# Gradients of keys, values and the input x in three interleaved stages, with memory rows padded to full tiles

## The chip, the cores and the metric

One core of one Trainium2 chip runs the whole program. The metric is the device time of one execution in microseconds, lower is better. The kernel before takes 8813.72 us (median of 4 runs beside the changed kernel).

## The reference, cut to what matters

The program computes a gated mix of two attentions over 2048 tokens, and all gradients. Branch A is attention with 32 heads and one set of keys and values. Branch B, which this change concerns, walks through 64 segments of 32 tokens; each segment attends to itself (causally) and to 8 memory rows that the segment before it wrote.

```python
for s in range(n_seg):
    xs = x[:, s * seg_len:(s + 1) * seg_len, :].copy()
    h = jnp.concatenate([mem, xs], axis=1)
    q, k, v = ...                       # projections of h, 32 heads of 128
    p = _softmax(masked scores, axis=-1)
    o = ...                             # p @ v, output projection to 576
    mem = o[:, :M, :].copy()
    outs.append(o[:, M:, :])
...
return g * a + (1 - g) * b              # then the gradients of all inputs
```

The stage at hand comes after the backward walk through the memory rows. For each tile of 128 tokens and each half of the heads (a **unit**; there are 16 x 2 = 32) it forms the gradients of keys and values as sums of two parts, from the tokens' own queries and from the memory rows' queries, stores them, transposes them, and multiplies the gradients of q, k and v by the transposed weights into the gradient of the input x.

## The kernel before

In the sums, the part of the tokens is a matmul over 128 rows, the part of the memory rows one over the 32 rows that belong to a group of four heads. They alternate, both adding into the same place:

```python
for tt in range(NTT):
    dxa = ...; load; dxa = gwb * dz + dxa                # gate's term, VectorE
    px = psum.tile([P, 640], F32, name="x_b", bufs=1)
    for r in range(2):
        # ... five loads of 512 KB, one buffer each; keys, values, memory rows
        for w, lt, rt, ml, mr, sc in (("v", ...), ("k", ...)):
            dt = sp.tile([P, 4, 4, E], BF16, name="g_dt", bufs=1)
            for g in range(4):
                rs = slice(32 * g, 32 * g + 32)
                pk = psum.tile([P, 4, E], F32, name="x_p", bufs=4)
                for i in range(4):
                    self.mm(pk[:, i, :], lhsT=lt[:, g, i, :], rhs=rt[:, g, i, :], start=True, stop=False)
                    self.mm(pk[:, i, :], lhsT=ml[rs, i, :], rhs=mr[rs, i, :], start=False, stop=True, tp=(32 * g, 0))
                nc.scalar.mul(dt[:, g], pk[:], sc)
                self.tr4(psum, "x_tr", lambda i: dt[:, g, i, :], de[:, g], use="v")
            nc.gpsimd.dma_start(self.DX[w][tok, hc], ...)
        for n, w in enumerate("qvk"):                    # input gradients, 16 heads each
            # ... 512 and 64 columns per head, added into px
    # ... dx = dxa + px, stored
```

The order of the instructions on each engine is set by the compiler's scheduler; some stages of this program fix TensorE's order by hand (`self.chain = True`), this one did not.

The softmax here doesn't subtract the row's maximum and nothing guards it: scores larger than these inputs give would overflow.

## Time and profile before

| | kernel before |
|---|---|
| median time | 8813.72 us |
| profiled execution | 8801.6 us |
| stage of this change | 7013.0 to 7970.3 us: 957.3 us, 29.9 us per unit |
| TensorE's granted clock in the stage | 0.78 |
| TensorE busy by the records | 953.98 us of 957.3 |
| DMA share, rate | 0.60, 183 GB/s |

The busy share of TensorE says little here, because each record is counted from start to a modelled end, and records overlap (in the prediction's timeline, records of 0.23 us start 0.16 us apart). What counts are the distances between starts, and the clock that the chip granted. The prediction below shows both.

### The profile page before, as it was taken

How to read it: one execution, taken by the hardware profiler on the slowest of the kernel's cores; microseconds unless marked ns; L12 is line 12 of the kernel's file. 1: busy time of each engine (PE TensorE's matmuls, PEld its weight loads, DVE VectorE, ACT ScalarE, POOL GpSimd, SP SyncE). 2: the span in 40 equal slices, each digit the busy share in tenths (PEclk: the TensorE clock that was granted, in tenths of full speed). 3: DMA queues.
4: the chain of work that ended last, by engine and by line, in shares of the span. 5: the costliest groups of instructions: out<-in, count | busy, mean ns of one | idle time of the engine just before them, and what ended most of it. 6: DMA issues, size and time to landing. Idle time of an engine off the chain costs nothing. (4 is left out here: it accounts for less than half of the span.)

```text
span 8801.6 us, 210293 instructions
## 1 busy us (share of the span) xinstructions
PE 8158.4 (93%) x89816; PEld 3903.5 (44%) x89816; DVE 4321.7 (49%) x6659; ACT 3835.0 (44%) x7412; POOL 1184.8 (13%) x3062
## 2 busy tenths in 40 slices
PE   6999999999999979978999899979999799997999
PEld 2222222222222234435555566647777555554444
DVE  4889898898888924432333455542222111113000
ACT  3788787787777823332222355542222111112000
POOL 4100001000010014420000133320000011112000
PEclk9999999999999989979999999989999877776999
DMA  2000000000000045542211588883333466666444
GB/s 89 1 6 1 6 6 1 6 1 6 6 1 1 1 146 230 231 178 86 60 59 59 175 267 263 260 284 104 99 98 97 167 189 190 185 187 221 149 149 144
DMA packets 615950, 969.83 MB, mean 110 GB/s; under 512 B 187545, under 2 KB 406946, under 8 KB 594850
## 3 DMA queue, kind: packets, MB, share of 16 engines
q1 hardware_dynamic: 540978, 672.32, 24.4%
q0 software_dynamic: 72720, 282.73, 8.6%
q8 instruction: 702, 11.50, 0.5%
q14 instruction: 238, 1.95, 0.1%
q10 hardware_dynamic: 1312, 1.33, 0.0%
HBM read 552.06 MB, written 404.10 MB: 109 GB/s over the span
## 5 line engine op out<-in xcount | busy, mean ns | idle before, releaser
L1355 DVE TENSOR_TENSOR a_U<-a_d,a_E 128x1024 bf16<-128x1024 f32 x2048 | 2474.3, 1224 | 302.3 <-ACT a_E L1350 233.1
L1350 ACT ACTIVATE a_E<-a_s 128x512 bf16<-128x512 f32 x4096 | 2237.5, 595 | 564.7 <-PE a_s L79 478.9
L79 PE MATMUL a_s<-a_qaug,a_kmask 128*128 128x512 bf16 x2048 | 704.1, 388 | 54.7 <-ACT a_tk L1432 24.5
L79 PE MATMUL a_s<-a_kmask,a_qaug 128*128 128x512 bf16 x2048 | 697.3, 384 | 25.9 <-ACT a_E L1350 9.6
L79 PE MATMUL w_acc<-w_col,w_h 128*128 128x512 bf16 (+1 forms) x2400 | 526.1, 381 | 0.9 <-DMA w_col<-dqx 0.9
L79 PEld LDWEIGHTS <-d_g 128*32 128x32 bf16 x18432 | 494.6, 97 | 26.4 <-issue 9.9
L63 DVE CAST p_tok<-p_pb 128x512 bf16<-128x512 f32 x384 | 265.3, 692 | 318.4 <-PE p_pb L79 318.4
L79 PE MATMUL a_d<-a_doT,a_vaugT 32*128 32x512 bf16 x2048 | 401.5, 389 | 0.1
L79 PE MATMUL a_d<-a_vaugT,a_doaT 32*128 32x512 bf16 x2048 | 397.6, 385 | 0.0
L65 ACT COPY p_em<-p_tr 128x512 bf16<-128x512 bf16 x384 | 225.0, 586 | 357.7 <-PE p_tr L84 357.5
L1442 POOL TENSOR_TENSOR a_otok<-a_tk,a_rl 128x144 bf16<-128x144 f32 x64 | 27.5, 429 | 2525.4 <-DVE a_rl L1441 2525.4
L79 PEld LDWEIGHTS <-w_h 128*128 128x128 bf16 (+1 forms) x2400 | 237.4, 100 | 289.4 <-issue 24.2
L79 PEld LDWEIGHTS <-a_vaugT 32*128 32x128 bf16 x2048 | 96.4, 91 | 572.7 <-issue 572.6
L79 PEld LDWEIGHTS <-a_doaT 32*128 32x128 bf16 x2048 | 95.9, 91 | 538.0 <-issue 537.6
L65 ACT CAST c_tm<-c_pb 128x512 bf16<-128x512 f32 x192 | 112.5, 586 | 471.4 <-PE c_pb L79 471.2
L1042 ACT ACTIVATE g_dt<-x_p 128x512 bf16<-128x512 f32 x256 | 142.7, 599 | 355.5 <-DMA dvx<-g_dt 216.0
L63 DVE CAST c_tm<-c_pb 128x512 bf16<-128x512 f32 x192 | 132.9, 692 | 313.6 <-PE c_pb L79 309.2
L63 DVE CAST w_o<-w_acc 128x512 bf16<-128x512 f32 (+1 forms) x60 | 41.4, 690 | 481.3 <-PE w_acc L79 448.6
L79 PEld LDWEIGHTS <-c_mT 128*32 128x32 bf16 x7680 | 187.9, 96 | 190.9 <-DVE c_mT L396 25.4
L79 PEld LDWEIGHTS <-a_kmask 128*128 128x128 bf16 x2048 | 125.1, 97 | 313.8 <-issue 305.9
L79 PEld LDWEIGHTS <-p_xT 128*128 128x128 bf16 (+1 forms) x1920 | 154.8, 97 | 218.0 <-issue 87.7
L65 ACT CAST w_o<-w_acc 128x512 bf16<-128x512 f32 (+1 forms) x60 | 35.1, 585 | 496.6 <-PE w_acc L79 496.6
(482 smaller groups left out, 13797.5 us busy)
## 6 DMA issues: line engine op xcount, KB each, us to landing
xt_k<-p_tok SPq DMA_DIRECT2D x16, 1024.0 KB, 4.0
xe_k<-p_em POOLq DMA_DIRECT2D x16, 1024.0 KB, 5.5
xs_k<-p_seg POOLq DMA_DIRECT2D x64, 256.0 KB, 4.3
xt_v<-p_tok SPq DMA_DIRECT2D x16, 1024.0 KB, 3.9
xe_v<-p_em POOLq DMA_DIRECT2D x16, 1024.0 KB, 5.6
xs_v<-p_seg POOLq DMA_DIRECT2D x64, 256.0 KB, 2.9
xt_q<-p_tok SPq DMA_DIRECT2D x16, 1024.0 KB, 4.2
xe_q<-p_em POOLq DMA_DIRECT2D x16, 1024.0 KB, 5.8
```

The lines of the kernel that those rows point to most:

```text
L63: nc.vector.tensor_copy(out, in_)
L65: nc.scalar.copy(out, in_)
L79: self.follow(self.nc.tensor.matmul(out, lhsT, rhs, start=start, stop=stop, tile_position=tp, skip_group_check=True))
L1042: nc.scalar.mul(dt[:, g], pk[:], sc)
L1350: nc.scalar.activation(ex[:, j, :], s[:, :], ACT.Exp, scale=SCALEA)
L1355: nc.vector.tensor_tensor(out=u[:], in0=d[:], in1=ex[:], op=ALU.mult)
L1442: nc.gpsimd.tensor_tensor(out=osl, in0=v[:, :, :, o0:o0 + DA], in1=rl[:].to_broadcast([P, 4, 2, DA]), op=ALU.mult)
```

## The change

The intent is to keep TensorE dense. The memory rows are copied into tiles that are zero outside their own 32 rows, so that each second matmul also uses all 128 rows. The work of a unit goes through three stages (sums of 4 heads; transposes of the step before; input gradients of the step before that), interleaved with the memory part of the next unit, in an enforced order. The five large loads come in halves with two buffers, the output accumulator has two, and the stores of the key and value gradients are issued by ScalarE instead of GpSimd.

```diff
+        pad = {}
+        for nm in ("mdo", "mq"):
+            pad[nm] = keep.tile([P, 4, 4, E], BF16, name="g_pad_" + nm)
+            nc.gpsimd.memset(pad[nm][:], 0.0)
@@ ... cut ... @@
+        def own_rows(U, nm, g):
+            rs = slice(32 * g, 32 * g + 32)
+            nc.scalar.copy(pad[nm][rs, g], U[nm][rs])
@@ ... cut ... @@
+        def sums(U, w, g):
+            lt, rt, ml, nm, sc = ("eq", "dot", "eM", "mdo", 1.0) if w == "v" else ("sq", "qt", "sM", "mq", SCALEB)
+            pk = bank([P, 4, E])
+            for i in range(4):
+                self.mm(pk[:, i, :], lhsT=U[lt, g // 2][:, g % 2, i, :], rhs=U[rt, g // 2][:, g % 2, i, :], start=True, stop=False)
+                self.mm(pk[:, i, :], lhsT=U[ml][:, i, :], rhs=pad[nm][:, g, i, :], start=False, stop=True)
+            if g % 2 == 0:
+                U["d" + w] = sp.tile([P, 2, 4, E], BF16, name="g_dt" + w, bufs=2)
+            dt = U["d" + w]
+            nc.scalar.mul(dt[:, g % 2], pk[:], sc)
+            if g % 2:
+                tok = slice(U["tt"] * P, (U["tt"] + 1) * P)
+                c0 = U["r"] * 2048 + (g // 2) * 1024
+                nc.scalar.dma_start(self.DX[w][tok, c0:c0 + 1024], dt[:].rearrange("p g i e -> p (g i e)"))
+            return dt[:, g % 2]
@@ ... cut ... @@
+        def prefetch(tt):
+            t = dxa[tt] = sp.tile([P, D], F32, name="g_dxa", bufs=2)
+            nc.sync.dma_start(t[:], self.dxA_dram[tt * P:(tt + 1) * P, :])
+            nc.vector.scalar_tensor_tensor(out=t[:], in0=gwb[:], scalar=self.dz_all[:, tt:tt + 1], in1=t[:],
                                            op0=ALU.mult, op1=ALU.add)
@@ ... cut ... @@
-                for w, lt, rt, ml, mr, sc in (("v", ld["eq"], ld["dot"], eM, mdo, 1.0), ("k", ld["sq"], ld["qt"], sM, mq, SCALEB)):
-                    dt = sp.tile([P, 4, 4, E], BF16, name="g_dt", bufs=1)
-                    de = sp.tile([P, 4, 4, P], BF16, name=f"g_d{w}e", bufs=1)
-                    for g in range(4):
-                        rs = slice(32 * g, 32 * g + 32)
-                        pk = psum.tile([P, 4, E], F32, name="x_p", bufs=4)
-                        for i in range(4):
-                            self.mm(pk[:, i, :], lhsT=lt[:, g, i, :], rhs=rt[:, g, i, :], start=True, stop=False)
-                            self.mm(pk[:, i, :], lhsT=ml[rs, i, :], rhs=mr[rs, i, :], start=False, stop=True, tp=(32 * g, 0))
-                        nc.scalar.mul(dt[:, g], pk[:], sc)
-                        self.tr4(psum, "x_tr", lambda i: dt[:, g, i, :], de[:, g], use="v")
-                    nc.gpsimd.dma_start(self.DX[w][tok, hc], dt[:].rearrange("p g i e -> p (g i e)"))
-                    em[w] = de
-                for n, w in enumerate("qvk"):
-                    for i in range(4):
-                        for g in range(4):
-                            h = 16 * r + 4 * g + i
-                            st, sp_ = n + r + i + g == 0, n == 2 and r == 1 and i + g == 6
-                            for lo, hi in ((0, 512), (512, D)):
-                                self.mm(px[:, lo:hi], lhsT=em[w][:, g, i, :], rhs=self.WT[w][:, h, lo:hi], start=st, stop=sp_)
@@ ... cut ... @@
+        for n, U in enumerate(units):
+            N = units[n + 1] if n + 1 < len(units) else None
+            if U["r"] == 0:
+                prefetch(U["tt"])
+            if N:
+                load_keys(N)
+            for g in range(4):
+                if g == 0:
+                    loads(U, 1)
+                if g == 2 and N:
+                    loads(N, 0)
+                if g == 3 and n + 2 < len(units):
+                    load_memory(units[n + 2])
+                for w in "vk":
+                    dt = sums(U, w, g)
+                    if N:
+                        if (g, w) == (0, "v"):
+                            memory_rows(N, "mdo", "do")
+                        if (g, w) == (0, "k"):
+                            memory_rows(N, "mq", "q")
+                        if (g, w) == (1, "k"):
+                            memory_scores(N)
+                        if (g, w) == (2, "k"):
+                            memory_gradients(N)
+                        own_rows(N, "mdo" if w == "v" else "mq", g)
+                    inputs(U, "q", g, (0, 1) if w == "v" else (2, 3), U["dqe", g // 2][:, g % 2])
+                    if done:
+                        done[-1].append(columns(done[-1][3]))
+                    if len(done) > 1:
+                        V, w2, g2, _, de = done.pop(0)
+                        inputs(V, w2, g2, range(4), de)
+                    done.append([U, w, g, dt])
+        done[-1].append(columns(done[-1][3]))
+        for V, w2, g2, _, de in done:
+            inputs(V, w2, g2, range(4), de)
+        self.chain = False
```

More of the change, by code (lines that the diff above doesn't have):

```diff
@@ L987, in b_x_gradients @@
         NTT = self.NTT
+        units = [dict(tt=tt, r=r) for tt in range(NTT) for r in range(2)]
         gwb = keep.tile([P, D], BF16, name="g_gwb")
         nc.sync.dma_start(gwb[:], self.gate_w.partition_broadcast(P))
-        for tt in range(NTT):
-            tok = slice(tt * P, (tt + 1) * P)
-            dxa = sp.tile([P, D], F32, name="g_dxa", bufs=2)
-            nc.sync.dma_start(dxa[:], self.dxA_dram[tok, :])
-            nc.vector.scalar_tensor_tensor(out=dxa[:], in0=gwb[:], scalar=self.dz_all[:, tt:tt + 1], in1=dxa[:],
-                                           op0=ALU.mult, op1=ALU.add)
-            px = psum.tile([P, 640], F32, name="x_b", bufs=1)
-            for r in range(2):
-                hc = slice(r * 2048, (r + 1) * 2048)
-                ld = {}
-                for nm, src in (("qt", self.XT["q"][tok, hc]), ("dot", self.DOX[tok, hc]), ("eq", self.EQ[tt, r]),
-                                ("sq", self.SQ[tt, r]), ("dqe", self.DQE[tt, r])):
-                    ld[nm] = sp.tile([P, 4, 4, P], BF16, name="g_" + nm, bufs=1)
-                    nc.sync.dma_start(ld[nm][:].rearrange("p a b n -> p (a b n)"), src)
-                ke = self.load_em(sp, "g_ke", self.XE["k"], tt, r, 1)
-                ve = self.load_em(sp, "g_ve", self.XE["v"], tt, r, 1)
-                me = self.load_me(sp, "g_me", self.ME, (0, 3), tt, r, 1)
-                mde = self.load_me(sp, "g_mde", self.DME, (0,), tt, r, 1)
-                mq = self.tok_me(sp, psum, "g_mq", me, 0)
-                mdo = self.tok_me(sp, psum, "g_mdo", mde, 0)
-                prm = sp.tile([P, 16, 32], BF16, name="g_prm", bufs=1)
-                nc.gpsimd.tensor_tensor(out=prm[:], in0=mde[:, 0], in1=me[:, 1], op=ALU.mult)
-                S = psum.tile([P, 4, P], F32, name="x_p", bufs=4)
-                self.mm(S[:].rearrange("p i n -> p (i n)"), lhsT=self.identB[:, :],
-                        rhs=self.maskM[:].rearrange("p i n -> p (i n)"), start=True, stop=False)
-                for i in range(4):
-                    for g in range(4):
-                        self.mm(S[32 * g:32 * g + 32, i, :], lhsT=me[:, 0, 4 * i + g, :], rhs=ke[:, g, i, :],
-                                start=False, stop=True, tp=(0, 32 * g))
-                eM = sp.tile([P, 4, P], BF16, name="g_eM", bufs=2)
-                nc.scalar.activation(eM[:], S[:], ACT.Exp, scale=SCALEB)
-                pp = psum.tile([P, 4, P], F32, name="x_p", bufs=4)
-                for i in range(4):
-                    for g in range(4):
-                        self.mm(pp[32 * g:32 * g + 32, i, :], lhsT=mde[:, 0, 4 * i + g, :], rhs=ve[:, g, i, :],
-                                start=True, stop=False, tp=(0, 32 * g))
-                    for g in range(4):
-                        self.mm(pp[32 * g:32 * g + 32, i, :], lhsT=prm[:, 4 * i + g, :], rhs=self.negonesB[:, :],
-                                start=False, stop=True, tp=(0, 32 * g))
-                sM = sp.tile([P, 4, P], BF16, name="g_sM", bufs=2)
-                nc.vector.tensor_tensor(out=sM[:], in0=pp[:], in1=eM[:], op=ALU.mult)
-                em = {"q": ld["dqe"]}
-                for w, lt, rt, ml, mr, sc in (("v", ld["eq"], ld["dot"], eM, mdo, 1.0), ("k", ld["sq"], ld["qt"], sM, mq, SCALEB)):
-                    dt = sp.tile([P, 4, 4, E], BF16, name="g_dt", bufs=1)
-                    de = sp.tile([P, 4, 4, P], BF16, name=f"g_d{w}e", bufs=1)
-                    for g in range(4):
-                        rs = slice(32 * g, 32 * g + 32)
-                        pk = psum.tile([P, 4, E], F32, name="x_p", bufs=4)
-                        for i in range(4):
-                            self.mm(pk[:, i, :], lhsT=lt[:, g, i, :], rhs=rt[:, g, i, :], start=True, stop=False)
-                            self.mm(pk[:, i, :], lhsT=ml[rs, i, :], rhs=mr[rs, i, :], start=False, stop=True, tp=(32 * g, 0))
-                        nc.scalar.mul(dt[:, g], pk[:], sc)
-                        self.tr4(psum, "x_tr", lambda i: dt[:, g, i, :], de[:, g], use="v")
-                    nc.gpsimd.dma_start(self.DX[w][tok, hc], dt[:].rearrange("p g i e -> p (g i e)"))
-                    em[w] = de
-                for n, w in enumerate("qvk"):
-                    for i in range(4):
-                        for g in range(4):
-                            h = 16 * r + 4 * g + i
-                            st, sp_ = n + r + i + g == 0, n == 2 and r == 1 and i + g == 6
-                            for lo, hi in ((0, 512), (512, D)):
-                                self.mm(px[:, lo:hi], lhsT=em[w][:, g, i, :], rhs=self.WT[w][:, h, lo:hi], start=st, stop=sp_)
-            dx = sp.tile([P, D], BF16, name="g_dx", bufs=2)
-            nc.vector.tensor_tensor(out=dx[:], in0=dxa[:], in1=px[:, 0:D], op=ALU.add)
-            nc.sync.dma_start(self.outs[1][tok, :], dx[:])
@@ new lines, in b_x_gradients, with half @@
+        pad = {}
+        for nm in ("mdo", "mq"):
+            pad[nm] = keep.tile([P, 4, 4, E], BF16, name="g_pad_" + nm)
+            nc.gpsimd.memset(pad[nm][:], 0.0)
+        bank = lambda shape, dt=F32: psum.tile(shape, dt, name="g_p", bufs=2)
+        flat = lambda t: t.rearrange("p a b -> p (a b)")
+        dxa, px, left = {}, {}, {}
+        def half(U, name, src, h):
+            tt, r = U["tt"], U["r"]
+            t = sp.tile([P, 2, 4, P], BF16, name="g_" + name, bufs=2)
+            cs = slice(h * 1024, h * 1024 + 1024)
+            nc.sync.dma_start(t[:].rearrange("p g i n -> p (g i n)"),
+                              src[tt * P:(tt + 1) * P, r * 2048 + h * 1024:r * 2048 + h * 1024 + 1024] if len(src.shape) == 2 else src[tt, r][:, cs])
+            U[name, h] = t
@@ new lines, in loads, with load_memory @@
+        def loads(U, h):
+            half(U, "eq", self.EQ, h)
+            half(U, "dot", self.DOX, h)
+            half(U, "dqe", self.DQE, h)
+            half(U, "sq", self.SQ, h)
+            half(U, "qt", self.XT["q"], h)
+        def load_memory(U):
+            tt, r = U["tt"], U["r"]
+            U["q"] = self.load_me(sp, "g_me", self.ME, (0,), tt, r, 2)
+            U["do"] = self.load_me(sp, "g_mde", self.DME, (0,), tt, r, 2)
+            U["o"] = self.load_me(sp, "g_mo", self.ME, (3,), tt, r, 1)
+            U["prm"] = sp.tile([P, 16, 32], BF16, name="g_prm", bufs=1)
+            nc.gpsimd.tensor_tensor(out=U["prm"][:], in0=U["do"][:, 0], in1=U["o"][:, 0], op=ALU.mult)
@@ new lines, in load_keys, with memory_rows @@
+        def load_keys(U):
+            U["ke"] = self.load_em(sp, "g_ke", self.XE["k"], U["tt"], U["r"], 1)
+            U["ve"] = self.load_em(sp, "g_ve", self.XE["v"], U["tt"], U["r"], 1)
+        def memory_rows(U, nm, src):
+            t = U[nm] = sp.tile([P, 4, E], BF16, name="g_" + nm, bufs=1)
+            ptr = psum.tile([P, 4, P], BF16, name="g_tr", bufs=2)
+            for i in range(4):
+                self.tr(ptr[:, i, :], U[src][:, 0, 4 * i:4 * i + 4, :].rearrange("p g m -> p (g m)"), P)
+            nc.scalar.copy(t[:], ptr[:])
@@ new lines, in own_rows, with memory_scores @@
+        def own_rows(U, nm, g):
+            rs = slice(32 * g, 32 * g + 32)
+            nc.scalar.copy(pad[nm][rs, g], U[nm][rs])
+        def memory_scores(U):
+            S = bank([P, 4, P])
+            self.mm(flat(S[:]), lhsT=self.identB[:, :], rhs=flat(self.maskM[:]), start=True, stop=False)
+            for i in range(4):
+                for g in range(4):
+                    self.mm(S[32 * g:32 * g + 32, i, :], lhsT=U["q"][:, 0, 4 * i + g, :], rhs=U["ke"][:, g, i, :],
+                            start=False, stop=True, tp=(0, 32 * g))
+            U["eM"] = sp.tile([P, 4, P], BF16, name="g_eM", bufs=2)
+            nc.scalar.activation(U["eM"][:], S[:], ACT.Exp, scale=SCALEB)
@@ new lines, in memory_gradients @@
+        def memory_gradients(U):
+            pp = bank([P, 4, P])
+            for i in range(4):
+                for lt, rt, first in ((U["do"][:, 0], U["ve"], True), (U["prm"], None, False)):
+                    for g in range(4):
+                        self.mm(pp[32 * g:32 * g + 32, i, :], lhsT=lt[:, 4 * i + g, :],
+                                rhs=rt[:, g, i, :] if first else self.negonesB[:, :], start=first, stop=not first, tp=(0, 32 * g))
+            U["sM"] = sp.tile([P, 4, P], BF16, name="g_sM", bufs=2)
+            nc.vector.tensor_tensor(out=U["sM"][:], in0=pp[:], in1=U["eM"][:], op=ALU.mult)
@@ new lines, in sums @@
+        def sums(U, w, g):
+            lt, rt, ml, nm, sc = ("eq", "dot", "eM", "mdo", 1.0) if w == "v" else ("sq", "qt", "sM", "mq", SCALEB)
+            pk = bank([P, 4, E])
+            for i in range(4):
+                self.mm(pk[:, i, :], lhsT=U[lt, g // 2][:, g % 2, i, :], rhs=U[rt, g // 2][:, g % 2, i, :], start=True, stop=False)
[9 more added lines that the diff above has]
+            return dt[:, g % 2]
@@ new lines, in columns, with inputs @@
+        def columns(src):
+            ptr = psum.tile([P, 4, P], BF16, name="g_tr", bufs=2)
+            for i in range(4):
+                self.tr(ptr[:, i, :], src[:, i, :], P)
+            de = sp.tile([P, 4, P], BF16, name="g_de", bufs=3)
+            nc.vector.tensor_copy(de[:], ptr[:])
+            return de
+        def inputs(U, w, g, ii, src):
+            tt = U["tt"]
+            if tt not in px:
+                px[tt] = psum.tile([P, 640], F32, name="g_x", bufs=2)
+                left[tt] = 3 * HB
+            for i in ii:
+                h = 16 * U["r"] + 4 * g + i
+                st = left[tt] == 3 * HB
+                left[tt] -= 1
+                for lo, hi in ((0, 512), (512, D)):
+                    self.mm(px[tt][:, lo:hi], lhsT=src[:, i, :], rhs=self.WT[w][:, h, lo:hi], start=st, stop=left[tt] == 0)
+            if left[tt] == 0:
+                dx = sp.tile([P, D], BF16, name="g_dx", bufs=1)
+                nc.vector.tensor_tensor(out=dx[:], in0=dxa.pop(tt)[:], in1=px.pop(tt)[:, 0:D], op=ALU.add)
+                nc.sync.dma_start(self.outs[1][tt * P:(tt + 1) * P, :], dx[:])
@@ new lines, in prefetch @@
+        def prefetch(tt):
+            t = dxa[tt] = sp.tile([P, D], F32, name="g_dxa", bufs=2)
+            nc.sync.dma_start(t[:], self.dxA_dram[tt * P:(tt + 1) * P, :])
+            nc.vector.scalar_tensor_tensor(out=t[:], in0=gwb[:], scalar=self.dz_all[:, tt:tt + 1], in1=t[:],
+                                           op0=ALU.mult, op1=ALU.add)
+        U = units[0]
+        load_memory(U)
+        load_keys(U)
+        loads(U, 0)
+        load_memory(units[1])
+        self.chain = True
@@ new lines, in b_x_gradients @@
+        memory_rows(U, "mdo", "do")
+        memory_rows(U, "mq", "q")
+        for g in range(4):
+            own_rows(U, "mdo", g)
+            own_rows(U, "mq", g)
+        memory_scores(U)
+        memory_gradients(U)
+        done = []
+        for n, U in enumerate(units):
[4 more added lines that the diff above has]
+                load_keys(N)
+            for g in range(4):
+                if g == 0:
[23 more added lines that the diff above has]
+                    done.append([U, w, g, dt])
```

## The prediction

> **What bounds the kernel now.** I began with the page's slices, because the change touches one stage only. The tile view of the stage's output accumulation puts its matmuls from 7006.1 to 7970.3 us, slices 31 to 36 of 40.
>
> ```profile
> PE   6999999999999979978999899979999799997999
> PEclk9999999999999989979999999989999877776999
> DMA  2000000000000045542211588883333466666444
> ```
>
> There PE is at 9, DMA at 6, and the granted clock at 7: the lowest long stretch of the kernel. The second view is the table of stretches for this stage (columns: start:end, us, then busy us of PE, PEld, DVE, ACT, POOL, clock, DMA share, GB/s), with four pieces of it:
>
> ```profile
> 7013.00:7970.30 957.30, 953.98 (x7931) 516.12 (x7923) 159.79 (x350) 179.84 (x320) 163.61 (x469) 0.78 0.60 183
> ...
> 7301.00:7309.00 8.00, 8.00 (x69) 4.10 (x66) 0.00 (x0) 0.00 (x0) 0.00 (x0) 1.00 0.42 123
> 7311.00:7315.00 4.00, 4.00 (x32) 2.46 (x31) 1.02 (x3) 1.19 (x2) 3.31 (x11) 1.00 0.79 244
> 7316.00:7328.00 12.00, 12.00 (x59) 5.72 (x59) 1.57 (x3) 2.66 (x5) 1.13 (x2) 0.50 0.63 197
> ```
>
> The stage is 957.3 us for 32 units (16 token tiles, two halves of the heads), 29.9 us a unit. DVE, ACT and POOL are each under 20% busy. Inside a unit the clock is 1.00 for some microseconds and then exactly 0.50. Third view, TensorE's waits in the stage:
>
> ```profile
> PE x_b L79 <- DMA g_dqe<-dqe: 43.1, 1, 43.1
> PE x_p L79 <- ACT g_eM L1021: 0.2, 1, 0.2
> ```
>
> Only the first load is waited for. So no buffer, evacuation or transfer holds TensorE afterwards; it holds itself. Fourth view, its timeline in one unit (start, duration, engine, line, operation, count), shows how:
>
> ```profile
> 7301.12 4.08 PE L79 MATMUL x_b<-WTv,g_dve 128*128 128x512 bf16 x32
> 7305.04 4.08 PE L79 MATMUL x_b<-WTk,g_dke 128*128 128x512 bf16 x32
> 7308.96 0.39 PE L84 MATMUL x_tr<-identB,g_me 128*128 128x128 bf16 x4
> 7309.18 0.39 PE L84 MATMUL x_tr<-identB,g_mde 128*128 128x128 bf16 x4
> ...
> 7312.42 0.23 PE L79 MATMUL x_p<-g_mdo,g_eM 32*128 32x128 bf16 x1
> 7312.58 0.23 PE L79 MATMUL x_p<-g_dot,g_eq 128*128 128x128 bf16 x1
> 7312.74 0.23 PE L79 MATMUL x_p<-g_mdo,g_eM 32*128 32x128 bf16 x1
> ...
> 7322.24 0.29 PE L79 MATMUL x_p<-g_qt,g_sq 128*128 128x128 bf16 x1
> 7322.46 0.28 PE L79 MATMUL x_p<-g_mq,g_sM 32*128 32x128 bf16 x1
> 7322.68 0.29 PE L79 MATMUL x_p<-g_qt,g_sq 128*128 128x128 bf16 x1
> ```
>
> Durations overlap, so starts must be compared. Four transposes take 0.22 us (7308.96 to 7309.18): 55 ns for 128 columns. Sixteen heads of input gradients take 3.92 us: 245 ns for a 512- and a 64-column matmul. But in the key and value sums, where a full 128-row matmul and a 32-row one alternate, starts are 160 ns apart at full clock and 215 ns later, for the same 128 columns.
>
> I added the start-to-start distances of all the stage's matmuls, by group. Per unit: input gradients 13.5 us (96 matmuls; 11.8 at the warm rate), sums 12.0 us (64, on average 188 ns), transposes of the gradients 2.9 us (32), memory part 1.5 us. Sum 29.9.
>
> **What the Trainium skill says.** "TensorEngine Tiling (Array Packing)", Key Properties: changing the tiling mode (not just the tile) drains TensorE. The trace agrees: 160 ns apart where the mode changes at each matmul, 55 where it doesn't. "TensorE: Matmul & The Clock Gate", section "What's actually happening": the clock gate has two states, half and full rate, set by how busy the array has recently been, in windows of about 3.4 us. The trace agrees with the two states, 0.50 and 1.00, and the 0.50 begins some 4 us after the sparse sums begin, though every record calls PE busy. The same page, "Why this matters for your kernels": a single K=32 matmul costs as much as one with K=128, only concurrency gains. So zero padding should cost no TensorE time; no run here shows that yet. "DMA: Bandwidth & Descriptors", "Issuing engines are not separate DMA queues": transfers from SP, ACT and POOL share the same 16 engines. So moving stores to ACT saves issue time on POOL and no bandwidth.
>
> **The change, part by part.**
>
> *Padding.* The memory rows of each group of heads are copied into a tile that is zero elsewhere; the second matmul of each pair uses all 128 rows. The count stays 64 per unit, but the mode no longer changes. 64 x 56 ns = 3.6 us instead of 12.0: minus 8.4 us. Both matmuls still write one place in turn, but this costs nothing: in the backward chain a matmul and the next one adding onto it start 55 ns apart (6934.54 and 6934.59 us).
>
> *Clock.* With sums dense, nothing sparse is left, so I expect about 1.00. Input gradients become 48 x 245 ns = 11.8 us (minus 1.7). Gradient transposes become 32 x 56 ns = 1.8 us (minus 1.1; some of theirs was a mode change too).
>
> *Memory part.* Same matmuls, but scores and gradients now stand apart: two more mode changes of some 0.1 us (160 less 55). 1.5 becomes 1.75 us.
>
> Unit: 3.6 + 11.8 + 1.8 + 1.75 = 18.9 us of TensorE.
>
> *Copies into the padding.* Eight of ACT per unit, 32 partitions x 512. Estimate: the 0.59 us of a 128 x 512 copy, as the row length is the same. ACT per unit: 8 scalings x 0.60, 2 copies x 0.59, one exponential 0.60, 8 paddings x 0.59, 4 store issues of some 0.4 (as SP's) = 12.9 us, 68%. Beside TensorE, not on its path.
>
> *Three stages in fixed order.* Each step of 2.1 us does sums of 4 heads, transposes of the step before, input gradients of the one before that. A 0.60 us scaling has about 2.6 us before its transposes are due. DVE needs 8 x 0.43 + 0.69 + 0.78 = 4.9 us per unit. I expect few waits from these, but the order is now fixed, so a late result stops TensorE where before another group could fill in.
>
> *Loads.* In halves, double-buffered. Key, query-side and output loads are the same bytes. The memory load takes two of four kinds instead of all four, so 256-byte packets fall from 2560 to 1536 per unit.
>
> **DMA, the tightest other limit.** The stage keeps DMA 0.60 busy, 17.9 us per unit. After: 9 x 512 KB in 2 KB packets is 2304 packets; in the x-attention stage such packets took 104 ns on average (5000 to 5800 us, where DMA was 0.82 busy), so 15.0 us over 16 engines. Plus 1536 x 18 ns / 16 = 1.7 and about 0.8 for the rest: 17.5 us. Against 18.9 that is over 90%; close. For it: in x-attention at 263 GB/s TensorE's longest waits name ACT and DVE, none a transfer. This stage would need 5.3 MB / 19.5 us = 272 GB/s. Against: loads wait in order behind 12 small memory loads on SP, and half a unit's loads can be asked for only when the last sums have let their buffer go. I add 0.85 us per unit for such stalls: 19.75 us.
>
> *Edges.* The first loads still wait behind the 14 MB of weights (TensorE idle until about 7006 to 7013). The new order needs two units' memory rows first and ends in a short pipeline tail: plus 8 us.
>
> Sum: 957.3 - 32 x 19.75 = 325 us saved, less 8 = 317. 8812.75 - 317 = 8495.
>
> **Rivals.**
> 1. *DMA becomes the bound.* Speaks for it: over 90% by my count. Against: packets took 159 ns at the median for 4 KB but 215 on average, so much of the 17.9 us is queueing. If so, about 22 us a unit: 704 us, saved some 245, 8565.
> 2. *The clock stays low* (power, or waits that keep the array sparse). For: the stage is at 0.78 now. Against: the dense weight gradients run 600 us at 1.00. Then 18.9 / 0.78 = 24.2 us a unit: saved 175, 8640.
> 3. *Evacuation waits in the fixed order:* two banks for sums, ACT at 68% in order. X-attention, built likewise, lost 55 us of 800 to such waits. That is 7%, or 1.3 us a unit; 8510 if it adds to half my allowance.
> 4. *The 160 ns are not mode changes*, but the pairwise accumulation. Then the padding gives nothing, and only half the clock's effect could return: within 2%. The 55 ns in the backward chain speaks against.
>
> **Range and chances.** 18.9 us a unit without stalls and with the edges gone gives 957.3 - 605 = 352 saved, 8461; somewhat better if the start is hidden, 8445. 22 us a unit with edges gives 8565; high end 8575. Faster by over 2% needs 176 us, or 24.4 us a unit: only rivals 2 and 4 fail it. 0.95 faster, 0.04 same, 0.01 slower.
>
> **What would show it.** Right: starts in the sums about 56 ns apart; clock of the stage 0.95 or more; units of 19 to 20.5 us; DMA near 0.85 to 0.9 and 260 to 275 GB/s; TensorE's waits small. Wrong: waits on the half loads (rival 1), clock near 0.78 with dense starts (2), waits on the scaled sums, exponentials or padding copies (3), sums still 160 ns apart (4). Other stages should not move by more than a few us.

## More of the kernel before

One view of the kernel before that it did not use became important later, ScalarE's waits in the stage (engine, line, what it waited for, us in total, times, longest):

```profile
ACT g_dt L1042 <- DMA dvx<-g_dt: 216.0, 31, 8.2
```

ScalarE waits 216 us for the store of the last gradient rows, because their tile has one buffer. TensorE did not wait for ScalarE, so it cost nothing then.

## The result, and the profile after

| | before | after |
|---|---|---|
| median | 8813.72 us (8796.3 to 8819.1) | 8524.66 us (8512.93 to 8529.97) |
| profiled execution | 8801.6 us | 8511.2 us |
| stage | 957.3 us | 676.7 us (7005.0 to 7681.7) |
| per unit | 29.9 us | 21.1 us |

The ratio is 0.9674, with a 95% interval of 0.9657 to 0.9690. A ratio here is the mean time of one kernel's fast runs over the mean of the other's of the same rounds, so it is not quite the ratio of the medians. The medians differ by 289 us; 317 had been predicted, and 8524.66 lies inside the range of 8445 to 8575.

Nearly all of it is in the stage: 957.3 - 676.7 = 281 us. Of the remaining 10 us between the two profiled executions, 8 are an earlier start of the sums (7005 instead of 7013). First, the table of stretches of the kernel after: the whole stage, a piece that runs undisturbed, a piece in which TensorE stands, and one just after it (columns as in the prediction):

```profile
7005.00:7681.70 676.70, 612.57 (x7783) 412.52 (x7910) 152.04 (x319) 351.80 (x597) 131.85 (x403) 0.97 0.83 250
7302.00:7320.00 18.00, 17.58 (x217) 11.91 (x214) 4.42 (x9) 10.83 (x19) 4.05 (x13) 1.00 0.79 244
7321.00:7325.00 4.00, 0.66 (x7) 0.41 (x8) 0.88 (x2) 0.69 (x2) 3.05 (x9) 1.00 0.98 258
7326.60:7330.00 3.40, 3.40 (x21) 1.95 (x19) 0.42 (x1) 1.21 (x2) 0.00 (x0) 0.51 0.83 230
```

The clock of the stage is 0.97 instead of 0.78 and DMA is 0.83 busy instead of 0.60. But the last two lines show a loss that the kernel before did not have: TensorE is busy 0.66 us of 4, and some microseconds later its clock is at about one half (the trace's clock records have 0.5 from 7326.5 to 7330.0 us). TensorE's timeline of the kernel after:

```profile
7301.48 0.24 PE L79 MATMUL g_p<-g_ve,g_mde 128*32 128x128 bf16 x4
...
7303.74 0.22 PE L79 MATMUL g_p<-g_dot,g_eq 128*128 128x128 bf16 x1
7303.80 0.22 PE L79 MATMUL g_p<-g_pad_mdo,g_eM 128*128 128x128 bf16 x1
7303.85 0.22 PE L79 MATMUL g_p<-g_dot,g_eq 128*128 128x128 bf16 x1
...
7320.37 0.24 PE L79 MATMUL g_p<-g_ve,g_mde 128*32 128x128 bf16 x4
```

Starts in the sums are 50 to 60 ns apart instead of 160 and 215. The first and last line are the same place of two successive units: 18.89 us apart. Of the 31 distances between successive units 11 are 18.89 us and none is shorter, the mean is 21.0. So that is what an undisturbed unit takes, and it is the 18.9 us that the prediction had added up. The stage takes more than 32 x 18.9 = 605 us, by 72 us. TensorE's waits in the stage name the largest part (as above: what waited, for what, us, times, longest):

```profile
PE g_x L79 <- DVE g_de L1082: 31.9, 13, 4.7
PE g_x L79 <- issue: 9.8, 61, 0.2
PE g_tr L84 <- ACT g_mdo L1034: 6.7, 4, 3.7
PE g_tr L84 <- POOL g_mde L438: 3.1, 1, 3.1
```

Thirteen times TensorE waits for `g_de`, the copy of transposed gradients by VectorE. VectorE's own timeline at one of them shows why the copy is late (in brackets: how long the engine sat idle before it, and what ended that):

```profile
7316.91 0.42 DVE L1082 COPY g_de<-g_tr 128x512 bf16<-128x512 bf16 x1 [2.38 <-PE g_tr L84]
7324.12 0.82 DVE L1105 SCALAR_TENSOR_TENSOR g_dxa<-g_gwb,dz_all,g_dxa 128x576 f32<-128x576 bf16 x1 [6.78 <-DMA g_dxa<-dxA_dram]
7324.85 0.42 DVE L1082 COPY g_de<-g_tr 128x512 bf16<-128x512 bf16 x1
```

The gate's operation on the loaded input gradient was put in front of the copy, its load had not landed, and VectorE stood for 6.78 us with TensorE's operand behind it. This comes once per token tile, every second unit. TensorE's order is fixed before the program runs, so it finds nothing else to do in the meantime (without the enforcement too: in e5_no_order it waits 40.3 us for `g_de`).

### The profile page after: what moved, and what is told of

Read it like the earlier page. It is cut to its first block, busy times and chain, and to the rows that moved or that the text cites. A ratio compares the mean times of both kernels' runs of the same rounds, so it can differ in the third digit from the quotient of the medians.

```text
span 8511.2 us, 210872 instructions
## 1 busy us (share of the span) xinstructions
PE 7768.0 (91%) x89300; PEld 3797.9 (45%) x89816; DVE 4315.6 (51%) x6627; ACT 4011.3 (47%) x7700; POOL 1153.9 (14%) x3000
## 5 line engine op out<-in xcount | busy, mean ns | idle before, releaser
L1082 DVE COPY g_de<-g_tr 128x512 bf16<-128x512 bf16 x256 | 108.3, 424 | 392.1 <-PE g_tr L84 391.2
L843 ACT ACTIVATE d_ET<-d_g 128x256 bf16<-128x256 f32 x64 | 24.5, 383 | 493.6 <-PE d_g L79 440.0
```

The source lines that it names most:

```text
L843: nc.scalar.activation(L["ET"][:, 1, :], S[:, :], ACT.Exp, scale=SCALEB)
L1082: nc.vector.tensor_copy(de[:], ptr[:])
```

## The experiments

Twelve kernels were run; all gave correct results. "Stage" is the time from the first sum to the last input gradient in the profiled execution, to about 1 us. The prediction's rivals were DMA as the bound, a clock that stays low, evacuation waits, and pairwise accumulation in place of mode changes; the runs also set the order and the buffers against the padding. "Clock" is TensorE's mean granted clock in the stage. The results in one table, in the order in which they are told:

| run | what it is | median us | ratio to before (95%) | stage us | clock |
|---|---|---|---|---|---|
| changed kernel | | 8524.66 | 0.9674 (0.9657 to 0.9690) | 676.7 | 0.97 |
| e2_pad_only | before + padding | 8721.3 | 0.9897 (0.9877 to 0.9917) | 865 | 0.93 |
| e4_before_grouped | before, sums grouped | 8710.21 | 0.9878 (0.9863 to 0.9893) | 849 | 0.92 |
| e9_pad_two_stores | before + padding + second store buffer | 8545.7 | 0.9701 (0.9685 to 0.9717) | 696.7 | 0.99 |
| e3_no_pad | after, no padding | 8672.73 | 0.9844 (0.9827 to 0.9860) | 820.3 | 0.99 |
| e8_no_pad_grouped | after, no padding, sums grouped | 8539.09 | 0.9693 (0.9679 to 0.9706) | 690.7 | 0.98 |
| e5_no_order | after, order not enforced | 8536.72 | 0.9691 (0.9677 to 0.9706) | 693 | 0.94 |
| e1_late_gate | after, gate's operation moved (in vain) | 8545.17 | 0.9691 (0.9673 to 0.9709) | 688.5 | 0.96 |
| e10_gate_after_sum | after, gate's operation after the sum | 8513.36 | 0.9665 (0.9650 to 0.9679) | 668.2 | 0.98 |
| e6_pool_stores | after, stores by GpSimd | 8524.8 | 0.9664 (0.9651 to 0.9677) | 672.0 | 0.97 |
| e11_gate_pool_stores | e10 and e6 together | 8488.75 | 0.9631 (0.9618 to 0.9644) | 637.8 | 0.98 |
| e7_keep_weights | e10, weights kept from the chain | 8485.59 | 0.9634 (0.9619 to 0.9648) | 667.1 | 0.98 |
| e12_keep_pool_stores | e10, e6 and e7 together | 8454.71 | 0.9598 (0.9585 to 0.9611) | 633.4 | 0.99 |

### Padding alone: e2_pad_only

```diff
+        pad[nm, r] = keep.tile([P, 4, 4, E], BF16, ...)      # zeroed once, one per half of the heads
+        nc.scalar.copy(pad["mdo", r][rs, g], mdo[rs])         # and the same for mq, for each g
-        self.mm(pk[:, i, :], lhsT=ml[rs, i, :], rhs=mr[rs, i, :], start=False, stop=True, tp=(32 * g, 0))
+        self.mm(pk[:, i, :], lhsT=ml[:, i, :], rhs=mr[:, g, i, :], start=False, stop=True)
```

> The kernel before with the padding alone: full-tile memory rows, old loads, old order. Theory (the mode change at each matmul of the sums is the main cost, and it is what halves the clock): starts in the sums about 56 ns apart, clock of the stage above 0.9, and the larger part of the gain: 8530 to 8625, with some new waits for loads that have one buffer only. Rival (order, halves and double buffers carry the gain): less than a third of it, above 8715.

It took 8721.3 us, 90 us less than the 8810.75 us of before in the same rounds. That is the rival's range, not the theory's: the sums became dense, yet two thirds of the gain stayed away. The waits of TensorE and then of ScalarE in its stage tell where the gain went:

```profile
PE x_tr L84 <- ACT g_dt L1051: 130.9, 33, 5.8
PE x_p L79 <- ACT g_eM L1030: 44.3, 32, 4.6
```

```profile
ACT g_dt L1051 <- DMA dvx<-g_dt: 247.8, 32, 9.4
```

In the kernel before TensorE waited 0.2 us for ScalarE in the whole stage; here it waits 175 us. ScalarE waits for the store of the last gradient rows, as it had done before, but before the slow sums had hidden it. The 44.3 us on `g_eM` are new too: ScalarE's exponential stands behind eight padding copies of 0.61 us (7317.8 to 7322.4 us in one unit). The clock records of these traces hold only 1.0 and 0.5; in the stage the clock was at 0.5 for 130 us, against 416 us before.

### The same with a second store buffer: e9_pad_two_stores

```diff
-        dt = sp.tile([P, 4, 4, E], BF16, name="g_dt", bufs=1)
+        dt = sp.tile([P, 4, 4, E], BF16, name="g_dt", bufs=2)
```

Against e2_pad_only it has this second buffer, and one padded tile of each kind instead of two, since otherwise it did not fit in SBUF.

> The padding alone in the kernel before, as e2_pad_only, with two buffers for the gradient rows that are stored (and one padded tile of each kind, to make room). Theory (padding alone gained only 90 us because ScalarE, with one buffer, waits for the store of the last gradient rows, and TensorE for ScalarE: 130.9 us of waits on g_dt): these waits fall below 40 us and the time to 8570 to 8640. Rival (the single-buffered loads are the real limit of the old order): waits move to the loads, above 8680.

It took 8545.7 us, even less than the range of the theory and only some 21 us more than the changed kernel. No wait on `g_dt` is left among TensorE's; the waits on `g_eM` remain (41.2 us), and the clock is 0.99. So padding plus one more buffer, in the old order and with the old single-buffered loads, gives most of what the whole rewrite gives. One padded tile less cannot well be the reason, since fewer buffers give more waits. That the loads have one buffer each did not hold TensorE: 2.9 us of waits on a load.

### Grouping instead of padding: e4_before_grouped

```diff
         for i in range(4):
-            self.mm(pk[:, i, :], lhsT=lt[:, g, i, :], rhs=rt[:, g, i, :], start=True, stop=False)
+            self.mm(pk[:, i, :], lhsT=lt[:, g, i, :], rhs=rt[:, g, i, :], start=i == 0, stop=False)
+        for i in range(4):
             self.mm(pk[:, i, :], lhsT=ml[rs, i, :], rhs=mr[rs, i, :], start=False, stop=True, tp=(32 * g, 0))
```

> The kernel before, with the four full and then the four 32-row matmuls of a sum together: 16 mode changes per unit instead of 64, same matmuls, no padding. Theory (about 104 ns per mode change, and the sparse sums halve the clock): sums 64 x 56 + 16 x 104 = 5.2 us per unit instead of 12.0, clock above 0.9, time 8550 to 8650. Rival (a 32-row matmul or a pair adding onto one place is slow in itself): above 8780. If pairwise accumulation alone were slow, this run would gain but the padding alone would not.

It took 8710.21 us: outside both ranges, again because of 125.2 us of new waits on `g_dt`. As evidence on the mode change it agrees with the theory: the same matmuls, of the same 32 rows, with a quarter of the changes, gained 100 us even behind that wait. A 32-row matmul that is slow in itself is excluded (the timeline of e8_no_pad_grouped, below, shows it directly). Pairwise accumulation is excluded by the changed kernel, where pairs still add into one place at 56 ns.

### The changed kernel without padding: e3_no_pad and e8_no_pad_grouped

```diff
-        self.mm(pk[:, i, :], lhsT=U[ml][:, i, :], rhs=pad[nm][:, g, i, :], start=False, stop=True)
+        self.mm(pk[:, i, :], lhsT=U[ml][rs, i, :], rhs=U[nm][rs, i, :], start=False, stop=True, tp=(32 * g, 0))
```

(with no padding copies, and two buffers for the memory rows that the next unit writes early)

> The changed kernel without the padding: the second matmul of each pair of the sums uses the 32-row tile again, all else as changed. Theory (mode changes): 160 ns between starts in the sums at full clock, 32 units x 64 x 104 ns = 213 us more, 8740, and up to 8840 if the clock falls to one half for stretches as before. Rival (the order and the buffers carry the gain): within 60 us of the changed kernel, below 8585.

It took 8672.73 us, 148 more than the changed kernel: less than the 213 of the theory, more than the 60 of the rival. Its stretch of the stage and its TensorE timeline:

```profile
7009.00:7829.30 820.30, 803.90 (x7783) 479.80 (x7911) 153.65 (x319) 201.06 (x349) 127.13 (x403) 0.99 0.70 207
```

```profile
7301.11 0.23 PE L79 MATMUL g_p<-g_dot,g_eq 128*128 128x128 bf16 x1
7301.27 0.23 PE L79 MATMUL g_p<-g_mdo,g_eM 32*128 32x128 bf16 x1
7301.43 0.23 PE L79 MATMUL g_p<-g_dot,g_eq 128*128 128x128 bf16 x1
```

Two things are seen. The 160 ns are back, so they belong to the alternation of modes and not to the old order. And the clock is 0.99 although the sums are as sparse as before: eight of them (1.3 us) now stand between dense matmuls, where the kernel before had all 64 in a stretch of nearly 14 us (7310.5 to 7324.4), with 16 transposes between. In the kernel before, the clock records go to 0.5 in every unit, 4.0 to 5.7 us after its sums begin; in e3_no_pad they hold one stretch at 0.5, at the start of the stage. So the clock did not need the padding; breaking up the sparse stretch was enough. The stage is 32 x (18.9 + 64 x 0.104) = 818 us by the prediction's terms and 820.3 by the trace: this kernel is bound by TensorE almost alone (nearly every unit takes 25.45 us, 64 x 103 ns more than 18.89), and the late operands that cost the changed kernel 72 us are nearly all hidden here. That is why it lost only 148 of the 213 us.

e8_no_pad_grouped does the four full and then the four 32-row matmuls, without padding.

> The changed kernel without padding, but with the four full matmuls of a sum and then its four 32-row ones: 16 mode changes per unit instead of 64, no padding copies on ScalarE. Theory (104 ns per mode change, nothing else): 16 x 104 ns x 32 = 53 us more TensorE work than the padded kernel, of which its waits for late operands take back a part: 8530 to 8580. Rival (the padding copies cost ScalarE time that TensorE waits for): faster than the changed kernel, below 8510.

It took 8539.09 us, inside the theory's range, and about as fast as the changed kernel (ratios 0.9693 and 0.9674, with overlapping intervals). Its timeline separates the two costs:

```profile
7300.43 0.39 PE L79 MATMUL g_p<-g_dot,g_eq 128*128 128x128 bf16 x4
7300.75 0.39 PE L79 MATMUL g_p<-g_mdo,g_eM 32*128 32x128 bf16 x4
7301.08 0.67 PE L79 MATMUL g_x<-WTq,g_dqe 128*128 128x512 bf16 x4
```

Four full matmuls take 0.32 us to the next start and four 32-row ones 0.33: four times 56 ns and one change of about 100 each. So a 32-row matmul takes as long as a full one, which the prediction had assumed and no run had shown, and the change costs extra. Undisturbed units take 20.45 us, 16 x 98 ns more than 18.89. The 16 mode changes per unit that are left cost 16 x 104 ns x 32 = 53 us of TensorE by the theory (50 by these units), but TensorE's waits on `g_de` fall from 31.9 to 13.9 us. Grouping, which costs no copies and no memory, would have served nearly as well as the padding.

### The enforced order: e5_no_order

```diff
         load_memory(units[1])
-        self.chain = True
         memory_rows(U, "mdo", "do")
```

> The changed kernel without the enforced TensorE order in this stage; program order, buffers and padding as changed. Theory (the stages in the program's order do the work, and the enforced order only repeats it): within 20 us of the changed kernel. Rival (the enforcement itself matters): over 40 us slower.

It took 8536.72 us, 12 us more than the changed kernel in the medians, with intervals that just overlap. Compared in the two traces by the tiles of TensorE's instructions, the scheduler keeps the same order by itself, apart from the first units. The structure of the program counts, the enforcement hardly.

### The wait on VectorE: e1_late_gate and e10_gate_after_sum

```diff
# e1_late_gate: in inputs(), just before dx = dxa + px, instead of in prefetch()
+        nc.vector.scalar_tensor_tensor(out=t[:], in0=gwb[:], scalar=self.dz_all[:, tt:tt + 1], in1=t[:], ...)
         nc.vector.tensor_tensor(out=dx[:], in0=t[:], in1=px.pop(tt)[:, 0:D], op=ALU.add)
```

> The changed kernel, but the vector operation that adds the gate's term to the loaded input gradient runs just before the final addition instead of when the load is asked for; same loads, same order on TensorE. Theory (VectorE, in order, stands behind the wait for that load once in two units, and the copies that TensorE needs stand behind it): the 31.9 us of TensorE waits on g_de fall below 5 us, the clock of the stage rises from 0.97 to 0.99 or 1.00, and the time falls by 35 to 50 us, to 8475 to 8490. Rival (the stage is limited by DMA at 0.84 busy, and the load is only where the shortage shows): the waits come back at the half loads, and the time falls by under 12 us.

It took 8545.17 us and showed nothing: the waits on `g_de` were 36.2 us, 13 times, as in the changed kernel. VectorE's records say why: the operation still stands directly behind its load (91.9 us of waits on it). Its only late input is that load, and the scheduler put it early again; moving it in the program did not move it on the engine. The run serves as a measure of noise instead: nearly the changed kernel once more, 20 us slower in the medians. Differences of medians below some 20 us between runs of different rounds are not read as effects here. So the next run let it depend on the result:

```diff
# e10_gate_after_sum
+        nc.vector.tensor_tensor(out=t[:], in0=t[:], in1=px.pop(tt)[:, 0:D], op=ALU.add)
+        nc.vector.scalar_tensor_tensor(out=dx[:], in0=gwb[:], scalar=self.dz_all[:, tt:tt + 1], in1=t[:], ...)
```

> The changed kernel with the gate's term added after the sum of loaded gradient and accumulated inputs, so that the operation needs the accumulated result and cannot be put early on VectorE (in e1_late_gate the compiler's ordering had put it back behind the load). Theory (VectorE stands behind that load once in two units): the 31.9 us of TensorE waits on g_de fall below 5 us, of the 38 us at half clock inside the stage most go, and the time falls by 35 to 50 us to 8475 to 8490. Rival (DMA at 0.84 busy is the limit and the shortage shows elsewhere): falls by under 12 us.

It took 8513.36 us. The waits on `g_de` are gone from the view, as the theory said, but the time fell by 11 us only, as the rival said (ratios 0.9665 and 0.9674: not distinguishable). TensorE's waits in its stage and ScalarE's timeline at one of them:

```profile
PE g_tr L84 <- ACT g_mdo L1034: 19.1, 20, 5.1
PE g_tr L84 <- ACT g_dtk L1070: 16.3, 13, 2.5
PE g_p L79 <- ACT g_dtk L1070: 4.3, 3, 3.1
```

```profile
7260.94 0.61 ACT L1038 COPY g_pad_mdo<-g_mdo 32x512 bf16<-32x512 bf16 x1
7264.62 0.33 ACTq L1074 DMA_DIRECT2D dvx<-g_dtv  x1
7265.00 0.60 ACT L1070 ACTIVATE g_dtk<-g_p 128x512 bf16<-128x512 f32 x1 [3.44 <-PE g_tr L84]
```

Some 40 us of waits on ScalarE have taken the place of 32 us on VectorE. ScalarE stands for 3.1 us from the end of a copy (7261.55) to the issue of a store, and the scaling that TensorE needs comes after the store.

### Stores by GpSimd: e6_pool_stores and e11_gate_pool_stores

```diff
-        nc.scalar.dma_start(self.DX[w][tok, c0:c0 + 1024], dt[:]...)
+        nc.gpsimd.dma_start(self.DX[w][tok, c0:c0 + 1024], dt[:]...)
```

> The changed kernel with the stores of the key and value gradients issued by GpSimd instead of ScalarE; the gate's operation stays where it was. Theory (two independent stops of TensorE, VectorE behind the gate's load and ScalarE behind its stores, of which one covers the other when both are there): TensorE's waits on g_de stay near 30 us, and the time falls by under 15 us against the changed kernel, to 8510 to 8525. Rival (the two add up: what both together gave, 36 us, less the 11 us of the gate alone): 25 us, 8495 to 8505.

> As e10_gate_after_sum, with the stores of the key and value gradients issued by GpSimd, as in the kernel before, instead of ScalarE. Theory (the transfers' queue is full at DMA 0.86, so the issue of a store blocks ScalarE for up to 5 us, and TensorE then waits for the scalings and copies behind it, 40 us in e10_gate_after_sum): these waits fall below 10 us, the clock rises to 0.99, and the time falls by 30 to 50 us against e10_gate_after_sum, to 8465 to 8485. Rival (DMA itself is the limit, and only the place of the wait moves, to the loads or to the rows' buffers behind GpSimd's copies): within 12 us of e10_gate_after_sum.

Alone, in the changed kernel, it gave nothing that can be told from noise (8524.8 us, ratio 0.9664 against 0.9674; 37.7 us of waits on `g_de`). Together with the gate's operation moved, it gave 8488.75 us, 36 us less than the changed kernel, somewhat short of the theory's 8465 to 8485. (Its profiled execution reached the stage some 26 us later than the others, so the stage's length, 637.8 us, compares better than that execution's total.) No wait on ScalarE is left among TensorE's in the stage; what remains are 24 us, 21 of them on loads (13.8 us on `g_dqe` alone). Each stop covers the other: with only one of them removed, TensorE meets the other. By the ratios each alone gave 8 to 9 us and both 38, with intervals of 11 to 15 us on each, so the waits show this more firmly than the times. Both removed, the loads appear, at a DMA share of 0.89.

What a store's issue by ScalarE waits for stands in the trace's instruction records, with the numbers of the semaphores, which the views leave out. Every transfer reports its landing to a semaphore (a counter). In this program the loads of SP and the stores of ScalarE take the same eight of them in turn, and before an issue the engine waits until the last transfer on that semaphore has landed; stores by GpSimd have eight of their own. In e10_gate_after_sum 69 of 127 store issues are held for over 0.3 us, 136 us in all and up to 5.6 us, and each time ScalarE goes on 0.02 us after a load by SP on the same semaphore has landed; 85 of the 136 us are for small loads of memory rows. In the changed kernel it is 37 issues and 57 us. One view shows it indirectly, among ScalarE's waits of e10_gate_after_sum:

```profile
ACT g_dtk L1070 <- DMA raw_g_me<-me: 60.0, 16, 5.7
```

The scaling does not read these rows; it stands behind a store that waits for them. So the theory of e11_gate_pool_stores had the right engine and the wrong reason: it is not a full queue but the landing of another engine's load. The change itself made this matter, with 28 transfers per unit on these eight semaphores (halved loads, memory loads by kind, stores) where the kernel before had 15.

### Weights kept, and all together: e7_keep_weights and e12_keep_pool_stores

The backward chain before this stage holds the same transposed weights in SBUF, in the same layout, and the stage loads them again. These kernels put them in a pool that outlives the chain:

```diff
-            WT[w] = wp.tile([P, HB, D], BF16, name=f"WTc{w}")
+            WT[w] = wt_pool.tile([P, HB, D], BF16, name=f"WT{w}")
...
             with SB("p4w") as p4w:
-                k.load_WT(p4w)
+                with SB("p4o") as p4o, SB("p4s") as p4s, PS("p4p") as p4p:
+                    k.b_chain_bwd(bk, p4o, p4s, p4p, p4w)
```

> As e10_gate_after_sum, and the transposed weights that the backward chain has already in SBUF are kept there, so that the 14 MB are not loaded a second time between the chain and this stage. Theory (TensorE idles 38.4 us at the start of the stage because its first loads stand behind the weights): this wait falls to about 10 us, 25 to 32 us less than e10_gate_after_sum, near 8450. Rival (the first memory rows come from the chain's last store and need that long anyway): under 8 us less.

> As e11_gate_pool_stores, with the weights kept from the backward chain. Theory: the start's 25 to 30 us come on top of it: 8435 to 8460, the shortest of all. Rival (DMA limit): within 12 us of e7_keep_weights, 8475 to 8495.

e7_keep_weights took 8485.59 us, 28 us less than e10_gate_after_sum, as expected, though not "near 8450", since e10_gate_after_sum itself had been expected lower. TensorE's first wait of the stage fell from 38.4 to 6.5 us. e12_keep_pool_stores took 8454.71 us, inside the theory's range, and is the fastest kernel: 0.9598 of before, against 0.9674 for the change as made. Its stage and its longest waits:

```profile
6983.60:7617.00 633.40, 613.12 (x7911) 406.98 (x7911) 152.48 (x318) 353.76 (x597) 196.66 (x531) 0.99 0.90 267
```

```profile
PE g_x L79 <- DMA g_dqe<-dqe: 11.5, 9, 2.8
PE g_tr L84 <- POOL g_mde L438: 4.4, 2, 3.3
PE g_p L79 <- DMA g_dot<-dox: 3.5, 2, 1.9
```

633.4 / 32 = 19.8 us per unit, 0.9 above TensorE's own 18.9. Most of what it still waits for are loads. Why these are late is not settled: the transfer engines are 0.90 busy, but SP's issues of loads are also held 161 us of the stage by the same eight semaphores (3 us in the kernel before), and no run changed that alone.

## Why the prediction was right or wrong

The prediction was right in size, 317 us forecast and 289 measured, and in most of its terms.

- **Mode change.** Right. 160 ns with alternating modes (kernel before, e3_no_pad), 56 ns without, grouping in between. In undisturbed units a change costs 103 ns (e3_no_pad) and 98 ns (e8_no_pad_grouped), and e3_no_pad's stage agrees with the sum to 2 us (818 and 820.3).
- **The unit of 18.9 us.** Right: 18.89 us in the undisturbed piece.
- **Clock.** The size was right (0.78 to 0.97; "about 1.00" was forecast), the reason only in part. The prediction tied it to dense sums. The runs show that either is enough: dense sums in the old order (e9_pad_two_stores, 0.99), or sparse sums in short pieces in the new one (e3_no_pad, 0.99). So what halved the clock before was the long sparse stretch: it needs the sparse sums and the old order together.
- **Who earns it.** The prediction took the padding for the main part and gave order and buffers no number of their own. Padding alone gave 90 us and the rest alone 138 (8810.75 - 8672.73), together 289. The padding needed a second buffer for the stored rows. The sign was in the profile of before: 216 us of waits of ScalarE for that store, which the prediction passed over because TensorE waited for nothing.
- **Stalls.** This is the term that was mis-sized: "I add 0.85 us per unit for such stalls: 19.75 us". Measured: (676.7 - 605) / 32 = 2.2 us per unit. In the changed kernel's waits the half loads, which the allowance was for, are hardly to be seen (2.4, 1.8 and 0.4 us). The largest is VectorE behind the gate's load, which the prediction did not think of: it counted VectorE's 4.9 us of work per unit, and not that a waiting instruction holds everything behind it. The clock lost after each stop comes on top: at 0.97, (1 - 0.97) / 0.5 x 676.7 = 41 us were at half speed, which costs about half of that. Waits of some 50 us (without the "issue" ones, which undisturbed units have too) and 20 us of clock make up the 72. 1.4 us too little per unit are 45 us.
- **Edges.** Forecast 8 us lost; measured some 5 gained: from the chain's last matmuls to the first sum 46.5 us (6958.4 to 7004.9), before 51.8 (6961.9 to 7013.7). The other runs agree: 46 to 48 us in the new order, 52 to 54 in the old, where the weights are loaded again. 317 - 45 + 13 = 285, near the measured 289. That two errors had opposite signs is luck.
- **DMA.** The share was forecast at 0.85 to 0.9 and measured at 0.83, 250 GB/s instead of 260 to 275, because the unit was longer; the DMA time per unit, 0.83 x 21.1 = 17.5 us, was the forecast one. Rival 1, that DMA becomes the bound at 22 us a unit, is refuted in that size: e12_keep_pool_stores runs 19.8 us a unit with DMA 0.90 busy at 267 GB/s. But e11_gate_pool_stores and it show loads as what TensorE waits for most. So loads are the next limit, as the prediction said; whether by the engines' speed or by the semaphores, no run shows.
- **Rival 3,** evacuation waits of about 1.3 us a unit, was nearest in number: its 8510 is a slip (18.9 + 0.43 + 1.3 us a unit and the edges give about 8524), and the measured median is 8525. In mechanism it was not: it expected waits for the scaled sums and the copies of ScalarE, which are 8.5 us here, and not an operation of VectorE behind a load.

What remains open is how much of the last 28 us in e12_keep_pool_stores (633.4 - 605) could be had with other load orders, or with fewer and larger loads on the eight semaphores.

## What to carry to other kernels

Before counting on the gain of a removed cost, list the waits of all engines in that stage, including those that cost nothing now: the 216 us that ScalarE stood behind a store became TensorE's wait (131 us in e2_pad_only) as soon as the sums were fast. On an engine that feeds TensorE, an instruction that waits for a load, or an issue of a transfer that waits for its semaphore, holds every copy behind it (6.78 and up to 5.6 us at a time here). Make the operation depend on something late, since moving it in the program may not move it on the engine; look up which transfer an issue waits for. And when one stop is removed and nothing is gained, look for the second one behind it before giving up the first: here each fix alone gave 0 to 11 us in the medians, both gave 36.

## What the Trainium skill lacked or had wrong

- "TensorEngine Tiling (Array Packing)", Key Properties, says that a mode change drains TensorE, without a cost. Here it was about 104 ns per change: 160 ns between starts with a change at each 128-column matmul, 56 without.
- "TensorE: Matmul & The Clock Gate", "Why this matters for your kernels", ties the half clock to idle gaps of over 3 us, and its section "A second HAM failure mode: psum-queue depth-cycling" to micro-idles between groups of matmuls; neither names mode changes. Here the clock fell to 0.50 with no gap, TensorE being recorded busy 12.00 of 12 us, in a long run of matmuls 160 ns apart; the same spacing in pieces of 1.3 us between dense matmuls left it at 0.99.
- "DMA: Bandwidth & Descriptors", "Issuing engines are not separate DMA queues", says that the issuing engine only changes who spends the (usually small) time of the issue. Here the issuing engine also decided what an issue waits for: SP and ScalarE share eight landing semaphores in this program, GpSimd has eight others. With the gate's operation moved, 69 of ScalarE's issues were held, 136 us in all, until loads of SP had landed, and taking the issues off it gave 25 us (8513.36 to 8488.75).
- No page read here treats as a cost that the compiler's scheduler may put an operation ahead of its place in the program and so directly behind a late load. In e1_late_gate VectorE stood 91.9 us for such loads, 16 times, and TensorE 36.2 us behind it.
